# Sixteen partitions of one weight piece loaded from GpSimd's queue, dealt to chosen DMA engines

## The chip, the core and the metric

The kernel runs on one core of one Trainium2 chip. A core has five engines that run side by side, each with an instruction stream of its own: TensorE (PE in the profile; PEld is its loading of weights), VectorE (DVE), ScalarE (ACT), GpSimd (POOL) and SyncE (SP), which here does nothing but issue DMA transfers. The transfers themselves are carried out by 16 DMA engines, which all queues share. Engines wait for each other on semaphores. The metric is the time of one execution on the device, in microseconds (us); lower is better.

## The reference

One decoding step of a transformer block for two tokens (batch B = 2, one position each), everything in float32:

```
xn = layernorm(x)                                   # x: 2 x 512
q  = xn @ wq                                        # wq: 512 x 4096, 32 heads of 128
s[b,h,:] = q[b,h] . k_cache[b,h,:,:] / sqrt(128)    # 8192 cached positions per head
o[b,h]   = softmax(s[b,h,:]) @ v_cache[b,h,:,:]
s  = o @ wo                                         # wo: 4096 x 512
g  = silu( gelu(layernorm(xn) @ w1 + b1) @ w2 + b2 )   # 512 -> 1376 -> 512
out = x + s * g
```

The two caches are 268 MB each; with the weights, 559 MB are read once. wo, which this change is about, is 8 MB.

## The kernel before

**Tiling.** The 64 pairs of batch and head are taken two at a time, which gives N = 32 turns. The 128 partitions are two heads of 64 partitions each, with 128 cached positions per partition. A turn's K or V tile is then 128 partitions by 64 KB, 8 MB, and one transfer. K tiles go alternately to the buffers `kb0` and `kb1`, V tiles to the one buffer `vb`.

**A turn.** VectorE multiplies the K tile by the query (line 524) and sums over the head's 128 numbers (line 531), which gives the scores. The maximum is found over the partitions with the help of PE, ScalarE takes the exponentials into PZ (line 552), and PE multiplies PZ with the V tile, 64 matmul records a turn (line 575, tile `po`). ScalarE copies the product out (line 582). The maximum and the product of turn n are done while the scores of turn n + 1 are formed.

**The end.** The last turn's V tile does not go to `vb` but, in two halves, to `kb1`. When PE has done with `vb` for the last time, wo is loaded into it. wo lies as `wo_sb[partition, c, column]` with 32 rows c of 512 columns for each partition, cut by `WO_PIECES = (0, 16, 24, 29, 31, 32)` into pieces of 16, 8, 5 and 2 rows, and the last row in two parts of 384 and 128 columns. The pieces have semaphores of their own, so PE starts on each as it lands: the first 24 rows with 512 columns at once into `wide` (line 650, 48 records), the others into `acc` (line 659, 64 records). VectorE multiplies by the gate g and adds x (lines 667 and 668), SP stores the result (line 669) and waits until it has landed (line 125).

**What sets the order.** The program is a list of operations (`op`), each with the tiles that it reads and writes; `Plan` derives the waits from these and hands each engine its own operations in the order of the list. All transfers are issued by SP in that order (`load`, line 314), so that each waits until its buffer is free, and those behind it wait too. GpSimd sets four tiles at the start and does nothing after that. `busy` issues matmuls whose result nobody reads (line 562).

**What the change touches.** The loads of wo near the end of `decode_kernel`, the products into `wide`, three new tiles' declarations, and the final wait in `Plan.emit`.

Of the kernel before, what the change touches and what calls it, by code (L numbers as in the profile page):

```python
# [21 lines left out]
class Plan:  # L22
# [18 lines left out]
    def op(self, eng, fn, r=(), w=(), over=(), it=None, loop=False, dma=None):  # L41


        o = Op()
        o.eng, o.fn, o.it, o.loop, o.dma, o.tell = eng, fn, it, loop, dma, False
        need = {}

        def after(d, war):
            if d.dma is None and dma is None and d.eng == eng and (eng == "pe" or war):
                return  # L50
            if d.dma is None:
                if need.get(d.eng) is None or need[d.eng].idx < d.idx:
                    need[d.eng] = d
            else:
                k = ("dma", d.dma)
                if need.get(k) is None or need[k].idx < d.idx:
                    need[k] = d

        for k in r:
            if k in self.writer:  # L60
                after(self.writer[k], False)
        for k in list(w) + list(over):
            if k in self.writer:
                after(self.writer[k], False)
            for d in self.readers.get(k, ()):
                after(d, True)
        clock = self.clock[eng]
        need = {k: d for k, d in need.items() if clock.get(k, 0) < d.idx}
        o.deps = [(k, d) for k, d in need.items()
                  if not any(e is not d and e.done.get(k, 0) >= d.idx for e in need.values())]  # L70
        for _, d in o.deps:
            for k, v in d.done.items():
                clock[k] = max(clock.get(k, 0), v)
        own = eng if dma is None else ("dma", dma)
        self.count[own] = o.idx = self.count.get(own, 0) + 1
        o.done = dict(clock)
        o.done[own] = o.idx
        for k in w:
            self.writer[k] = o
            self.readers[k] = []  # L80
        for k in r:
            if k not in w:
                self.readers.setdefault(k, []).append(o)
        self.ops.append(o)

    def emit(self, heads):

        nc = self.nc
        for o in self.ops:
            for _, d in o.deps:  # L90
                d.tell = True
        sems, value, told = {}, {}, {}
        for o in self.ops:
            key = o.eng if o.dma is None else ("dma", o.dma)
            if key not in sems:
                sems[key] = nc.alloc_semaphore(o.eng if o.dma is None else f"dma_{o.dma}")

            step = 16 if o.dma is not None else int(o.tell or o.eng != "pe")
            told[key] = told.get(key, 0) + step
            value[id(o)] = told[key]  # L100
        for o in self.ops:
            o.waits = {k: value[id(d)] for k, d in o.deps}

        def put(o, waits, turn=None):
            e = self.eng[o.eng]
            for k, v in waits:
                e.wait_ge(sems[k], v)
            i = o.fn() if o.it is None else o.fn(o.it if turn is None else turn)
            if o.dma is not None:
                i.then_inc(sems[("dma", o.dma)], 16)  # L110
            elif o.tell or o.eng != "pe":
                i.then_inc(sems[o.eng], 1)

        def order(d):
            return sorted(d.items(), key=lambda kv: str(kv[0]))

        for e in self.eng:
            ops = [o for o in self.ops if o.eng == e]
            inside = [j for j, o in enumerate(ops) if o.loop]
            if not inside:  # L120
                for o in ops:
                    put(o, order(o.waits))
                if e == "sp":

                    nc.sync.wait_ge(sems[("dma", "out")], told[("dma", "out")])
                continue
            for o in ops[:inside[0]]:
                put(o, order(o.waits))
            turns = {}
            for j in inside:  # L130
                turns.setdefault(ops[j].it, []).append(ops[j])
            n, m = len(turns), len(turns[1])
            assert inside == list(range(inside[0], inside[-1] + 1)) and list(turns) == list(range(1, n + 1))
            assert all(len(t) == m for t in turns.values())


            body, ahead = [], {}
            for j in range(m):
                col = [turns[i][j] for i in range(1, n + 1)]
                assert len({o.tell for o in col[1:-1]}) == 1, j  # L140
                for o in col:
                    o.tell = col[1].tell
                ws = []
                for k in sorted(set().union(*(o.waits for o in col)), key=str):
                    if all(k not in o.waits for o in col[1:]):
                        ahead[k] = max(ahead.get(k, 0), col[0].waits[k])
                        continue
                    step = col[2].waits[k] - col[1].waits[k]
                    base = col[1].waits[k] - 2 * step
                    for o in col:  # L150
                        assert o.waits.get(k) == step * o.it + base or (o.it == 1 and k not in o.waits), \
                            (e, j, k, o.it, [x.waits.get(k) for x in col])
                    ws.append((k, step, base))
                body.append((col[1], ws))
            for k, v in order(ahead):
                self.eng[e].wait_ge(sems[k], v)
            et = self.eng[e].engine
            with nc.Fori(1, n + 1, 1, engines=bass.OrderedEngineSet([et]), head_slot={et: heads[e]}) as i:
                for o, ws in body:
                    put(o, [(k, i * step + base if base else i * step) for k, step, base in ws], i)  # L160
            for o in ops[inside[-1] + 1:]:
                put(o, order(o.waits))


def decode_kernel(nc, x, kc, vc, wq, wo, w1, b1, w2, b2, out):
    P = 128
# [10 lines left out]
    QT = 4  # L177
# [19 lines left out]
    op = plan.op  # L197
# [13 lines left out]
    def sbuf(name, shape):  # L211
        return nc.alloc_sbuf_tensor(name, shape, F32).ap()

    def psum(name, shape):
        return nc.alloc_psum_tensor(name, shape, F32).ap()
# [5 lines left out]
    vb = sbuf("vb", [P, KP * DH])  # L221
# [3 lines left out]
    wo_sb = vb.rearrange("p (c n) -> p c n", c=OC)  # L225
# [28 lines left out]
    q_nat = O4  # L254
    rl = sbuf("rl", [P, B])
    on = sbuf("on", [P, RM, OC])


    used = [0]
# [14 lines left out]
    at = used[0]  # L274
# [23 lines left out]
    wide = psum("wide", [P, D])  # L298
# [4 lines left out]
    def bank():  # L303
        i = turn[0] % 4
        turn[0] += 1
        return scratch[i], f"s{i}"
# [6 lines left out]
    def load(dst, src, sem, w, over=()):  # L313
        op("sp", lambda: nc.sync.dma_start(dst, src), (), w, over=over, dma=sem)  # L314
# [9 lines left out]

    WO_PIECES = (0, 16, 24, 29, 31, 32)
    WIDE = WO_PIECES[-4]
    CUT = D - P


# [51 lines left out]
    for j in range(QT):  # L381
        pe(lambda j=j: matmul(px[R * j:R * j + RM, :P], pick, x_sb[:, j * P:(j + 1) * P],
                              start=True, stop=True), ["pick", "x"], [kx])
# [92 lines left out]
    for i in range(NQ):  # L476
        for c in range(ND):
            wv = wq_sb[:, c, :].rearrange("p (h s d) -> p h s d", s=U, d=DH)
            a = (NQ - 1 - i) * B
            for j in range(QT):  # L480
# [4 lines left out]
                    start=(i + c == 0), stop=(i == NQ - 1 and c == ND - 1)),  # L485
                   ["xnT"] + [("kb", 0, s) for s in range(2)], ["po"])
    act(lambda: nc.scalar.copy(q_nat, PO), ["po"], ["o4"])
    for k in range(N // NB):

        b, e = divmod(k, HH // NB)  # L490
        i, g = divmod(e, GQ)
        p, kp = bank()
        for s in range(U):
            a = R * (U * g + s) + B * i + b
            pe(lambda p=p, s=s, a=a: matmul(p[HP * s:HP * (s + 1), :], ident[:, a:a + 1].to_broadcast([P, HP]), q_nat,
                                            start=True, stop=True), ["ident", "o4"], [kp])
# [121 lines left out]

    wo_r = wo.rearrange("(p c) n -> p c n", p=P)
    for i, (a, e) in enumerate(zip(WO_PIECES[:-1], WO_PIECES[1:-1])):  # L620
        load(wo_sb[:, a:e], wo_r[:, a:e], f"wo{i}", [("wo", i)], over=["vb"])
    for i, (a, e) in enumerate(((0, CUT), (CUT, D)), len(WO_PIECES) - 2):
        load(wo_sb[:, OC - 1, a:e], wo_r[:, OC - 1, a:e], f"wo{i}", [("wo", i)], over=["vb"])

    max_dve(N - 1)
    exps(N - 1)
# [17 lines left out]
    def piece(c, j=0):  # L644
        return ("wo", max(i for i, a in enumerate(WO_PIECES[:-1]) if a <= c) + int(c == OC - 1 and j * P >= CUT))


    for c in range(WIDE):
        j = c % QT
        pe(lambda c=c, j=j: matmul(wide[R * j:R * j + RM, :], on[:, :, c], wo_sb[:, c, :],  # L650
                                   start=(c < QT), stop=(c + QT >= WIDE)), ["on", piece(c)], ["wide"])
    w4 = O4
    act(lambda: nc.scalar.copy(w4, wide), ["wide"], ["o4"])

# [7 lines left out]
    for j in range(QT):  # L662
        pe(lambda j=j: matmul(acc[R * j:R * j + RM, :], mod[:, :RM], w4[:, j * P:(j + 1) * P], start=True, stop=False),
           ["mod", "o4"], ["acc"])
    rows(WIDE, OC)

# [32 lines left out]
```

## Time and profile before

| what | value |
|---|---|
| median of 3 runs | 1299.35 us (1299.26 to 1299.38) |
| profiled execution | 1299.24 us |
| span of its instructions | 1297.9 us |
| VectorE busy | 1134.3 us, 87% of the span |
| PE busy | 404.1 us, 31% |
| GpSimd busy | 1.4 us, 8 instructions |
| read from memory | 559.30 MB, 431 GB/s over the span |

The span runs from the first to the last instruction; the profiled execution's own time is 1.34 us longer. The profile gives for each stretch of time the engines' busy times, the mean busy share of the 16 DMA engines and the rate at which they moved bytes. A packet of the trace carries its size and time, but not the number of its DMA engine. Entries like `vb<-in_A_wo_dram` read as destination and source. "Us to landing" is the time from the issue of a transfer to its last byte, so it includes the time in the queue behind earlier transfers.

### The profile page before, as it was taken

What the parts mean: (1) busy time and instruction counts of PE and PEld (TensorE: products, weight loads), DVE (VectorE), ACT (ScalarE), POOL (GpSimd) and SP (SyncE); (2) the same over time, 40 slices, a digit from 0 to 9 for tenths busy, and PEclk for the clock granted to TensorE, in tenths of its full rate; (3) what the DMA queues carried; (4) which work ended last, traced back from release to release, by engine and by line L of the source; (5) the groups of instructions that cost most, each with busy time, mean ns of one, the idle gap of its engine ahead of it and who ended that gap; (6) DMA issues with size and microseconds to landing.
All of it is one profiled execution on the core that took longest, in us unless ns stands there. A gap on an engine that the chain in (4) does not pass through costs nothing.

```text
span 1297.9 us, 6789 instructions
## 1 busy us (share of the span) xinstructions
PE 404.1 (31%) x2728; PEld 122.4 (9%) x2728; DVE 1134.3 (87%) x276; ACT 77.7 (6%) x250; POOL 1.4 (0%) x8
## 2 busy tenths in 40 slices
PE   5603333312333311333321333321333321233337
PEld 1201110000101100101100101000001100001102
DVE  2499999988889988889988888988888988888991
ACT  1200000000000000000000000000000000000000
POOL 0000000000000000000000000000000000000000
PEclk9856666656666656666656666655666655666659
DMA  9999999999999999999999999999999999999998
GB/s 408 443 423 442 430 430 438 424 446 426 436 432 426 444 426 440 428 434 436 426 446 426 434 434 424 446 426 438 430 432 438 426 446 426 434 434 424 433 432 366
DMA packets 11087, 559.45 MB, mean 431 GB/s; under 512 B 1236, under 2 KB 1604, under 8 KB 1736
## 3 DMA queue, kind: packets, MB, share of 16 engines
q1 hardware_dynamic: 11080, 559.36, 99.7%
q8 instruction: 4, 0.07, 0.0%
q14 instruction: 3, 0.02, 0.0%
HBM read 559.30 MB, written 0.06 MB: 431 GB/s over the span
## 4 chain that ended last, share of the span: by engine, by line
DMA 68%; PE 24%; DVE 4%; issue 3%; ACT 0%; SPq 0%; DVEq 0%
DMA vb<-in_A_v_cache_dram 66%; PE po L575 21%; DMA vb<-in_A_wo_dram 2%; DVE sc L531 2%; DVE kb L524 1%; PE s L410 1%; DMA vb<-in_A_x_dram 1%; PE po L482 1%; PE s L452 0%; PE s L412 0%; PE acc L659 0%; DVE vb L418 0%; ACT L431 0%; PE s L459 0%; SPq L314 0%
## 5 line engine op out<-in xcount | busy, mean ns | idle before, releaser
L524 DVE TENSOR_TENSOR kb<-kb,Q 128x8192 f32<-128x8192 f32 x64 | 555.5, 8681 | 100.6 <-DMA kb<-in_A_k_cache_dram 91.4
L531 DVE TENSOR_REDUCE sc<-kb 128x64 f32<-128x8192 f32 x64 | 552.3, 8666 | 0.0
L575 PE MATMUL po<-vb,PZ 128*8 128x512 f32 x1984 | 280.7, 729 | 282.0 <-DMA vb<-in_A_v_cache_dram 279.4
L547 PE MATMUL s<-nm,srow 1*128 1x2 f32 x64 | 18.4, 355 | 359.5 <-DVE nm L541 359.5
L575 PEld LDWEIGHTS po<-vb,PZ 128*8 128x8 f32 x1984 | 56.3, 103 | 480.3 <-issue 477.5
L538 PE MATMUL s<-ident,mx 128*1 128x128 f32 x32 | 11.8, 369 | 203.6 <-DVE mx L535 203.6
L547 PEld LDWEIGHTS s<-nm,srow 1*128 1x128 f32 x64 | 15.7, 302 | 368.8 <-DVE nm L541 368.8
L582 ACT COPY o<-po 128x512 f32<-128x512 f32 x32 | 18.7, 585 | 521.6 <-PE po L575 521.6
L548 ACT COPY bias<-s 128x2 f32<-128x2 f32 x32 | 5.1, 160 | 628.2 <-PE s L547 628.2
L584 PE MATMUL s<-mod,o 128*128 128x2 f32 x256 | 33.6, 253 | 22.1 <-ACT o L582 22.1
L584 PEld LDWEIGHTS s<-mod,o 128*128 128x128 f32 x256 | 31.0, 191 | 51.4 <-ACT o L582 51.3
L552 ACT ACTIVATE PZ<-sc,bias 64x128 f32<-64x128 f32 x64 | 25.5, 399 | 1.8
L538 PEld LDWEIGHTS s<-ident,mx 128*1 128x1 f32 x32 | 2.5, 79 | 207.1 <-DVE mx L535 176.6
L590 DVE TENSOR_TENSOR Z<-blk,s 128x8 f32 (+1 forms) x32 | 5.2, 163 | 12.2 <-PE s L584 12.2
L418 DVE COPY vb<-vb 2x384 f32<-2x384 f32 x4 | 1.8, 501 | 15.9 <-ACT vb L414 15.9
L410 PE MATMUL s<-vb 128*2 128x512 f32 (+1 forms) x24 | 12.5, 675 | 0.3 <-ACT vb L375 0.3
L667 DVE TENSOR_TENSOR gate<-acc,gate 128x128 f32<-128x128 f32 x1 | 0.3, 291 | 13.3 <-PE acc L659 13.3
L552 ACT ACTIVATION_READ_ACCUMULATOR PZ<-sc,bias 64x1 f32 x64 | 11.8, 185 | 0.0
L535 DVE TENSOR_REDUCE mx<-sc 128x1 f32<-128x128 f32 x32 | 9.2, 286 | 1.1
L556 ACT ACTIVATE ZR<-half,rs 128x8 f32 (+1 forms) x32 | 9.6, 301 | 4.1
L541 DVE TENSOR_REDUCE nm<-s 1x2 f32<-1x128 f32 x32 | 8.7, 272 | 0.3 <-PE s L538 0.3
L575 PE MATMUL po<-kb,PZ 128*8 128x512 f32 x64 | 8.5, 686 | 1.4 <-ACT PZ L552 1.4
(88 smaller groups left out, 82.8 us busy)
## 6 DMA issues: line engine op xcount, KB each, us to landing
kb<-in_A_k_cache_dram SPq DMA_DIRECT2D x4, 4096.0 KB, 42.7
kb<-in_A_v_cache_dram SPq DMA_DIRECT2D x2, 4096.0 KB, 40.6
vb<-in_B_w_dram SPq DMA_DIRECT2D x2, 2752.0 KB, 12.2
vb<-in_A_wo_dram SPq DMA_DIRECT2D x1, 4096.0 KB, 20.2
vb<-in_A_wo_dram SPq DMA_DIRECT2D x1, 2048.0 KB, 24.7
vb<-in_A_wo_dram SPq DMA_DIRECT2D x1, 1280.0 KB, 27.3
vb<-in_A_wo_dram SPq DMA_DIRECT2D x1, 512.0 KB, 28.1
vb<-in_A_v_cache_dram SPq DMA_DIRECT2D x31, 29.5
```

The costliest lines, as they stand in the source:

```text
L410: pe(lambda f=f, w=w, ph=ph, c=c: matmul(ph[:B, :w], yT[:, c, :], w1_sb[:, c, f:f + w], start=(c == 0), stop=False), ["yT", "w1"], [k])
L482: pe(lambda i=i, c=c, wv=wv, a=a, j=j, hd=hd: matmul(PO[R * j:R * j + NQ * B, :].rearrange("m (h d) -> m h d", d=DH), xnT[:, c, a:a + NQ * ...
L524: vector(n, n, lambda n: nc.vector.tensor_tensor(out=k, in0=k, in1=cols(Q, n * DH, DH).unsqueeze(1).to_broadcast([P, M, DH]), op=ALU.mult) ...
L531: vector(n, n, lambda n: nc.vector.tensor_reduce(out=SC[:, s * M:(s + 1) * M], in_=k, axis=AX.X, op=ALU.add), [("kb", i, s)], [("sc", s)])
L535: vector(n, n, lambda n: nc.vector.tensor_reduce(out=MX, in_=SC, axis=AX.X, op=ALU.max), [("sc", 0), ("sc", 1)], ["mx"])
L538: pe(lambda i: transpose(PM[:1, :P], MX, ident), ["mx", "ident"], ["s1"], it=n, loop=n > 0)
L547: pe(lambda i: matmul(PN[:, :U], srow, NM, start=True, stop=True), ["srow", "nm"], ["s2"], **one)
L552: act(lambda i, r=r, s=s: nc.scalar.activation(PZ[r, :, s, :], sc[r], AF.Exp, bias=BIAS[r, s:s + 1], scale=SCALE, accum_out=RS[r]), ["bias ...
L556: act(lambda i: nc.scalar.activation(cols(ZR, i * UP - UP, UP), half, AF.Copy, scale=RS), ["half"] + [("rs", s) for s in range(U)], [("ZR" ...
L575: pe(lambda i, t=t, j=j, v=v: matmul(PO[R * j:R * j + U * JW, :], PZ[:, t].rearrange("p s j -> p (s j)"), v[:, t * JW:(t + 1) * JW, :].rea ...
L582: act(lambda i: nc.scalar.copy(O4, PO), ["po"], ["o4"], **one)
L584: pe(lambda i, k=k: matmul(PT[:, :U], O4[:, k * DH:(k + 1) * DH], mod[:, k:U * JW:JW], start=(k == 0), stop=(k == JW - 1)), ["o4", "mod"], ...
```

## The change

The first piece of wo (16 rows c of 512 columns, 32 KB a partition) is no longer one transfer over 128 partitions. SP loads partitions 0 to 111 of it. Partitions 112 to 127 are loaded by GpSimd in six transfers: seven partitions, six partitions, and the last three partitions in four quarters of 8 KB each. The list `DEAL` has a positive number for such a transfer and a negative one for a small load into a tile `unused`, whose data nobody reads. The numbers are chosen so that, if each transfer of n rows takes the next n of the 16 DMA engines in turn, the rows come out on particular engines; the sizes of the list add up to a multiple of 16. Counted that way from engine 0, the six skipped are 0 to 5, the seven rows go to 6 to 12, two are skipped (13, 14), the six rows go to 15 and 0 to 4, the quarters to 5 to 7, 8 to 10, 11 to 13 and 14, 15, 0, and 15 skipped lead back to 0.

Each of GpSimd's six transfers has a semaphore (`rest0` to `rest5`), and PE waits for all of them before it uses the first piece. Behind wo, SP issues 15 loads of 15 rows, 14 rows and so on down to one row of 128 bytes into a tile `marks`, which nobody reads either. At its end SP waits for these and for `unused` as well as for the stored result.

```diff
@@ Plan.emit @@
                 if e == "sp":
-                    nc.sync.wait_ge(sems[("dma", "out")], told[("dma", "out")])
+                    for k in ("mark", "unused", "out"):
+                        nc.sync.wait_ge(sems[("dma", k)], told[("dma", k)])
@@ decode_kernel @@
+    unused = sbuf("unused", [16, 8 * 8])
+    TAG = 32
+    marks = sbuf("marks", [P, 15 * TAG])
...
     WIDE = WO_PIECES[-4]
+    REST = 16
+    DEAL = (-6, 7, -2, 6, 3, 3, 3, 3, -15)
...
     for i, (a, e) in enumerate(zip(WO_PIECES[:-1], WO_PIECES[1:-1])):
-        load(wo_sb[:, a:e], wo_r[:, a:e], f"wo{i}", [("wo", i)], over=["vb"])
+        n = P if i else P - REST
+        load(wo_sb[:n, a:e], wo_r[:n, a:e], f"wo{i}", [("wo", i)], over=["vb"])
+    spare = [0]
+    def some(p, n, a, e, i):
+        op("pool", lambda: nc.gpsimd.dma_start(wo_sb[p:p + n, a:e], wo_r[p:p + n, a:e]), (), [("wo", "rest", i)],
+           over=["vb"], dma=f"rest{i}")
+    def skip(n):
+        i = spare[0]
+        spare[0] += 1
+        op("pool", lambda: nc.gpsimd.dma_start(unused[:n, i * 8:i * 8 + 8], wo_r[:n, 0, :8]), (), [("unused", i)],
+           over=["vb"], dma="unused")
+    cut, at, row = WO_PIECES[1], 0, P - REST
+    assert sum(abs(k) for k in DEAL) % 16 == 0
+    lo, step = 0, cut // 4
+    for k in DEAL:
+        if k < 0:
+            skip(-k)
+        elif k < P - row:
+            some(row, k, 0, cut, at)
+            row, at = row + k, at + 1
+        else:
+            some(row, k, lo, lo + step, at)
+            lo, at = lo + step, at + 1
+    assert lo == cut
+    RESTS = [("wo", "rest", i) for i in range(at)]
     for i, (a, e) in enumerate(((0, CUT), (CUT, D)), len(WO_PIECES) - 2):
         load(wo_sb[:, OC - 1, a:e], wo_r[:, OC - 1, a:e], f"wo{i}", [("wo", i)], over=["vb"])
+    for n in range(15, 0, -1):
+        load(marks[:n, (n - 1) * TAG:n * TAG], wq[:n, :TAG], "mark", [("mark", n)])
...
-                                   start=(c < QT), stop=(c + QT >= WIDE)), ["on", piece(c)], ["wide"])
+                                   start=(c < QT), stop=(c + QT >= WIDE)), ["on", piece(c)] + (RESTS if c < WO_PIECES[1] else []), ["wide"])
```

Lines move by the added ones: `load` goes from 314 to 318, the products into `wide` from 650 to 687, those into `acc` from 659 to 696, the store from 669 to 706.

GpSimd's stream, before, from its last instructions at the start of the program to its end (partitions x elements of a partition; 8192 elements are 32 KB):

```order
L343 MEMSET ident 128x128 [waits barrier_Pool_Activation_PE_DVE_SP_gather]
L344 ISA [waits pool]
L344 AFFINE_SELECT ident<-ident 128x128
L346 MEMSET vb 128x512
L347 MEMSET PZ 128x256
```

and with the change:

```order
L353 MEMSET vb 128x512
L354 MEMSET PZ 128x256
L639 DMA unused<-in_A_wo_dram 6x8 [waits pe]
L633 DMA vb<-in_A_wo_dram 7x8192
L639 DMA unused<-in_A_wo_dram 2x8
L633 DMA vb<-in_A_wo_dram 6x8192
L633 DMA vb<-in_A_wo_dram 3x2048 x4
L639 DMA unused<-in_A_wo_dram 15x8
```

Nine transfers now end the stream of GpSimd; the first waits for PE, as the first piece of wo does on SP.

SP's stream, before, from the last V tile's two halves to the end:

```order
L314 DMA kb<-in_A_v_cache_dram 128x8192 [waits dve] x2
L314 DMA vb<-in_A_wo_dram 128x8192 [waits pe]
L314 DMA vb<-in_A_wo_dram 128x4096
L314 DMA vb<-in_A_wo_dram 128x2560
L314 DMA vb<-in_A_wo_dram 128x1024
L314 DMA vb<-in_A_wo_dram 128x384
L314 DMA vb<-in_A_wo_dram 128x128
L669 DMA out_dram<-gate 112x128 [waits dve]
```

and with the change, up to the first of the 15 tiny loads:

```order
L318 DMA kb<-in_A_v_cache_dram 128x8192 [waits dve] x2
L318 DMA vb<-in_A_wo_dram 112x8192 [waits pe]
L318 DMA vb<-in_A_wo_dram 128x4096
L318 DMA vb<-in_A_wo_dram 128x2560
L318 DMA vb<-in_A_wo_dram 128x1024
L318 DMA vb<-in_A_wo_dram 128x384
L318 DMA vb<-in_A_wo_dram 128x128
L318 DMA marks<-in_A_wq_dram 15x32
```

The first piece has 112 rows in place of 128, and the 15 tiny loads stand between the last piece and the store.

PE's stream around its first products with wo, before:

```order
L636 MATMUL OA<-mod,Z 128x32 [waits dve]
L562 MATMUL s<-Q,ident 128x512 x3
L650 MATMUL wide<-vb,on 2x512 [waits dve,dma_wo0]
L650 MATMUL wide<-vb,on 2x512 x15
L650 MATMUL wide<-vb,on 2x512 [waits dma_wo1]
```

and with the change:

```order
L673 MATMUL OA<-mod,Z 128x32 [waits dve]
L569 MATMUL s<-Q,ident 128x512 x3
L687 MATMUL wide<-vb,on 2x512 [waits dma_rest4,dma_rest5,dma_rest3,dma_wo0,dma_rest2,dve,dma_rest1,dma_rest0]
L687 MATMUL wide<-vb,on 2x512 x15
L687 MATMUL wide<-vb,on 2x512 [waits dma_wo1]
```

The order of PE's work is the same; its first product with wo has six more waits.

## The prediction

> **What bounds the kernel now.** I read the page first, then the chain of waits from 1225 us on, then stretches of the last 40 us.
>
> The page of the kernel before, parts 2 and 4:
>
> ```profile
> DMA  9999999999999999999999999999999999999998
> GB/s 408 443 423 442 430 430 438 424 446 426 436 432 426 444 426 440 428 434 436 426 446 426 434 434 424 446 426 438 430 432 438 426 446 426 434 434 424 433 432 366
> ...
> DMA 68%; PE 24%; DVE 4%; issue 3%; ACT 0%; SPq 0%; DVEq 0%
> ```
>
> The 16 DMA engines are full in all 40 slices but the last. What the kernel loads cannot shrink by this change (the same 8 MB of wo are read), so the question is what the last slice does.
>
> Chain of waits, its end (start us, us, what):
>
> ```profile
> 1265.90 27.34 DMA vb<-in_A_wo_dram
> 1293.25 0.04 issue
> 1293.29 2.33 PE acc L659 x64
> 1295.62 0.02 issue
> 1295.64 0.30 DVE gate L667
> ```
>
> The end hangs on wo: its pieces are issued when the buffer vb comes free, the DMA queue needs until 1293.25 us for the first three, PE multiplies the rest as they land, and DVE and the store follow. The timeline of PE and SP there (start, duration, and in brackets the idle time before):
>
> ```profile
> 1265.06 2.96 SPq L314 DMA_DIRECT2D vb<-in_A_wo_dram  x6
> ...
> 1275.53 0.12 PEld L575 LDWEIGHTS po<-kb,PZ 128*8 128x8 f32 x8 [0.85 <-DMA kb<-in_A_v_cache_dram]
> ...
> 1285.31 3.62 PE L650 MATMUL wide<-vb,on 128*2 128x512 f32 x32 [0.74 <-DMA vb<-in_A_wo_dram]
> ...
> 1290.20 1.90 PE L650 MATMUL wide<-vb,on 128*2 128x512 f32 x16 [1.27 <-DMA vb<-in_A_wo_dram]
> ...
> 1295.02 0.29 PEld L659 LDWEIGHTS acc<-vb,on 128*2 128x2 f32 x8 [0.16 <-DMA vb<-in_A_wo_dram]
> ...
> 1296.29 0.35 SPq L669 DMA_DIRECT2D out_dram<-gate  x1
> ```
>
> So piece 0 lands at 1285.3, piece 1 at 1290.2, and the last waits for wo end near 1295.0. PE has only 0.74 and 1.27 us of idle time at the first two. Whatever delays the slowest DMA engine in the last pieces delays the end by as much.
>
> Stretches (us from the span's start, length, engines' busy times, then clock, DMA share, GB/s):
>
> ```profile
> 600.00:700.00 100.00, 30.56 (x219) 9.10 (x207) 89.04 (x19) 4.64 (x15) 0.00 (x0) 0.64 1.00 431
> 1264.10:1275.50 11.40, 7.45 (x55) 2.31 (x43) 4.39 (x4) 2.03 (x7) 0.00 (x0) 0.85 0.99 426
> 1275.50:1285.20 9.70, 9.07 (x60) 4.00 (x56) 0.56 (x3) 0.58 (x1) 0.00 (x0) 1.00 0.97 414
> 1293.20:1294.20 1.00, 0.91 (x37) 0.89 (x40) 0.00 (x0) 0.00 (x0) 0.00 (x0) 1.00 0.50 182
> 1294.20:1295.20 1.00, 1.00 (x38) 0.49 (x26) 0.00 (x0) 0.00 (x0) 0.00 (x0) 1.00 0.17 51
> ```
>
> In the steady part 431 GB/s over 16 engines is 26.9 GB/s each, with a share of 1.00: no engine loses anything to another. In the last 2 us the share falls to 0.50 and 0.17: some engines are done while a few still work. That is what dealing can win. The two shares are 0.67 us of work per engine; spread evenly it would end at 1293.9, some 1.3 us before 1295.2. **A gain is thus bounded by 1.3 us, 0.10%**, below the 0.2% (2.6 us of 1299.35) that a measurement of this kernel can tell from no change.
>
> **The change, part by part.**
>
> *Unit of price.* Piece 0 is 4096 KB in 128 rows, so a row is 32 KB, and at 26.9 GB/s one engine moves it in 1.22 us. Before, an engine has eight of them (9.7 us, the length of the stretch from 1275.50 to 1285.20).
>
> *Balance.* If the dealing works as written, every engine has seven rows from SP; counting the deal with its skipped engines, nine engines get 40 KB from GpSimd, four get 32 KB, and three get 8 KB. Three engines are thus lighter by 24 KB, 0.91 us, and nine heavier by 8 KB, 0.30 us. Whether the three are the late ones the trace does not show, since its packets carry no engine number. From -1.3 us (all of the loss above) to +0.3 us (the late ones among the nine); I take -0.3, since the heavier engines and the next latest take over soon.
>
> *The 112 rows.* Now an engine gets 7 rows and not 8, so the rows can no longer fall into the sixteen eights of every other load of vb and kb, and an engine can write next to partitions that another one is writing. The trace has one transfer over 112 rows, the final store:
>
> ```profile
> out_dram<-gate SPq DMA_DIRECT2D x1, 56.0 KB, 1.6
> ...
> q1 hardware_dynamic: 128, 0.06, 14.1%
> ```
>
> (the second row is that store's own stretch, 1296.3 to 1297.9: packets, MB, share of 16 engines). It is 512 bytes a row and goes the other way, so it says nothing on a collision of 32 KB rows. The bounds are therefore 0 (no row meets another; as in the 431 GB/s row) and all seven rows at half rate, 7 x 1.22 = 8.5 us. If a row meets one of another engine, the two share the way in and the later one is up to 1.22 us late. I take four meetings on the unluckiest engine, 4.9 us: a little over the middle, because an engine that is late goes on meeting the others' rows in the next pieces, and because only the worst of 16 engines counts.
>
> [...]
>
> *GpSimd's 16 rows.* The first real transfer sends seven neighbouring rows by seven engines at once, while SP's queue holds the last half of the V tile (which lands at 1275.5). [...] The lower bound is 0, since the bytes are only moved from one queue to another. [...]
>
> *Moved bytes.* GpSimd's rows overtake SP's backlog, 512 KB at 431 GB/s = 1.2 us. The V half of 1275.53 comes that much later, and PE's work behind it shifts by 1.2; 0.74 of it is eaten by the wait at 1285.31, the remaining 0.5 by the 1.27 at 1290.20. Without that cover it would be 1.2 us. Priced 0.
>
> *GpSimd's issuing.* Nine DMAs, waiting as SP does for PE to free vb. POOL issues none before; the nearest rows are SP's:
>
> ```profile
> L314 SPq DMA_DIRECT2D vb<-in_A_wo_dram x6: 328/428/435, 1265.1 to 1267.6; - x6
> ...
> SPq L669 <- DVE gate L668: 28.2, 1, 28.2
> ...
> L125 SPq EVENT_SEMAPHORE  x1: 17/17/17, 1297.9 to 1297.9; - x1
> ```
>
> (issue time in ns, min/median/max; SP's wait before the store; the wait that ends the program). At 0.43 us nine are 3.9 us, done by 1269. PE's first use is at 1285.31, so the eight up to the last row may take 20.2 / 8 = 2.5 us each before anything waits. Nothing is queued behind them on POOL. Priced 0, the slow case is a rival.
>
> *Six more waits* stand before PE's first product with wo; all PE work behind it waits for the latest of the seven pieces. Passed at once, each costs some 17 ns like the last row above, six 0.1 us; they stand in PE's idle 0.74 us. Priced 0.
>
> *Fifteen tiny loads.* 15 x 0.43 = 6.5 us of issuing on SP, from 1268.0 to 1274.5, inside its wait of 28.2 us for the store. They stand behind wo in the queue, at most 15 rows on one engine. By the store's row (14.1% of 16 engines over 1.6 us is 3.6 us for 128 packets, 28 ns each) 15 rows and 15 signals cost 0.85 us, after wo's last packet and before the store at 1296.29. Hidden; 0.85 us if the store had to queue behind them. The end's two added waits are for transfers that land before the store: 0.
>
> *Sum.* -0.3 + 4.9 + 2.4 = +7.0 us. The profiled execution took 1299.24 us (span 1297.9 and 1.34 around it), 0.11 under the median of 1299.35: **1306.3 us** against the median.
>
> **The rivals.**
>
> *Rows do not collide* (the other side: not slower). Place: piece 0, 1275.5 to 1285.2. Then only the balance term is left, 1299.35 - 0.3 = **1299.0**, between 1298.0 and 1299.7. It decides as soon as piece 0 lands by 1286.5 (1285.3 plus PE's 1.27 us) and the engines end no further apart than now. For it: every transfer in the trace moves at 26.9 GB/s per engine; against it: all of these but tiny ones have 128 rows, eight an engine.
>
> *GpSimd's rows come too late.* If each of the eight issues takes 3.5 us, not 0.43, the last is out at 1265.06 + 28 = 1293.1. PE's 48 products with wide (3.62 + 1.90 us) then end at 1298.6 in place of 1292.1, some 6.5 us later, which is nearly all seen at the end: **1305.8**. Below 2.5 us each it costs nothing. Nothing in the trace speaks for it but that POOL's price is unknown.
>
> *The dealing does not do what it says.* If each of GpSimd's transfers begins on the same first engine, the skipped loads move nothing, and three engines carry 32 + 32 + 4 x 8 = 96 KB where an even share is 32: 64 KB more, 2.4 us. On late engines that is +2.4, on the earliest (1.3 us ahead) +1.1: **1301.1** without collisions, within 0.2%. [...] No GpSimd transfer is in the trace to decide it.
>
> **How the numbers follow.** Collisions 0.55 (1306.3; its own range 1302 to 1314); no collisions 0.30; GpSimd late 0.06; wrong dealing 0.07; an unforeseen gain 0.02. Slower by over 0.2%: collisions nearly whole (0.54), late GpSimd, and a tail of the dealing: 0.61. Within 0.2%: 0.37. Faster: 0.02, since the balance cannot give 2.6 us. The top of collisions is all bounds together, 8.5 + 4.9 + 0.3 = 13.7 us, 1313.0. To hold 8 in 10 the range reaches over the case without collisions: 1298.6 to 1313.
>
> **What would show it.** For the 112 rows: piece 0 (then 3584 KB) lands well after 1285.3, the DMA share between 1275 and 1290 falls below 0.9, and the stretch in which it fades at the end grows from 2 us to 5 or more. For GpSimd's rows: the V half of 1275.53 comes over 1.2 us later. For the issuing: POOL's nine DMAs spread over more than 20 us, and PE's wait before wide names one of them. For the dealing: how far the tiny loads, of 15 engines down to one, land apart. I am wrong if piece 0 lands at 1285 to 1286 and the end is where it was, or if the loss stands with PE waiting for GpSimd while SP's pieces are in time.

## The result, and the profile after

The changed kernel takes **1318.9 us** (median of four runs, 1317.64 to 1319.58); the kernel before, on the same chip, 1299.37 (1299.26 to 1299.41). The ratio is 1.0149, 95% interval 1.0132 to 1.0167: 19.5 us slower. The profiled execution took 1318.48 us with a span of 1317.2. The direction was forecast, and so was the kind of loss, rows that get in each other's way; the sum itself, +7.0, is little over a third of what came, and the time lies outside the range.

The page of the kernel after, parts 2, 3 and 4:

```profile
DMA  9999999999999999999999999999999999999997
GB/s 422 419 441 422 440 442 422 442 432 430 442 420 442 436 428 440 420 442 442 422 442 428 434 442 420 442 432 432 440 420 442 438 426 440 426 436 430 434 337 208
...
q0 software_dynamic: 288, 0.53, 0.3%
...
DMA 70%; PE 25%; DVE 3%; issue 1%; ACT 0%; POOL 0%; SPq 0%; DVEq 0%
```

The busy share reads as before: nines, and one digit lower at the end. What fell is the rate beside it: the last two slices (33 us each) move 337 and 208 GB/s, where the kernel before had 432 and 366. The engines are as occupied as before and move less. GpSimd's queue, which was not there before, moved 0.53 MB.

Stretches of the kernel after, cut where the last V half, piece 0 from SyncE, and the last piece land (start and end, length, busy us of PE, PEld, DVE, ACT, POOL, then clock, DMA share, GB/s):

```profile
1264.40:1282.80 18.40, 8.15 (x55) 2.44 (x47) 4.34 (x4) 2.03 (x7) 4.73 (x9) 0.86 1.04 284
1282.80:1301.80 19.00, 11.54 (x56) 4.23 (x56) 0.56 (x3) 0.58 (x1) 0.00 (x0) 0.77 0.95 218
1301.80:1307.60 5.80, 2.71 (x16) 0.59 (x20) 0.00 (x0) 0.00 (x0) 0.00 (x0) 0.50 0.97 391
1307.60:1312.70 5.10, 4.39 (x44) 0.77 (x36) 0.00 (x0) 0.58 (x1) 0.00 (x0) 0.92 0.34 124
```

In the first two, 37 us long together, the share is 1.04 and 0.95 and the rate 284 and 218 GB/s. (The share adds up the packets' own times; where it passes 1, packets of one engine must have overlapped.) From 1301.8 on the rate is 391 again: the loss belongs to the V half and piece 0, while GpSimd's rows and the 112 rows are under way, and hardly to what follows.

The timeline of PE and SP in the kernel after:

```profile
1265.62 2.97 SPq L318 DMA_DIRECT2D vb<-in_A_wo_dram  x6
1268.64 33.66 SPq L318 DMA_DIRECT2D marks<-in_A_wq_dram  x15
...
1282.87 6.12 PE L582 MATMUL po<-kb,PZ 128*8 128x512 f32 x32 [6.69 <-DMA kb<-in_A_v_cache_dram]
...
1304.88 7.07 PE L687 MATMUL wide<-vb,on 128*2 128x512 f32 x48 [10.47 <-DMA vb<-in_A_wo_dram]
...
1315.53 0.34 SPq L706 DMA_DIRECT2D out_dram<-gate  x1
```

and the DMA issues of its last part (issuer, KB each, median us from issue to landing):

```profile
vb<-in_A_wo_dram SPq DMA_DIRECT2D x1, 3584.0 KB, 36.2
...
vb<-in_A_wo_dram POOLq DMA_DIRECT2D x1, 224.0 KB, 16.0
vb<-in_A_wo_dram POOLq DMA_DIRECT2D x1, 192.0 KB, 25.3
...
vb<-in_A_wo_dram POOLq DMA_DIRECT2D x4, 24.0 KB, 33.3
...
vb<-in_A_wo_dram SPq DMA_DIRECT2D x1, 64.0 KB, 44.6
...
unused<-in_A_wo_dram POOLq DMA_DIRECT2D x1, 0.2 KB, 6.8
```

So the delay builds up as follows. The V half lands at 1282.87 in place of 1275.53, **7.3 us late**. Piece 0 is issued at 1265.62 and lands 36.2 us later, at 1301.8 in place of 1285.3: 16.5 late, **9.2 more**. The last piece, the sixth of SyncE's issues, starts at 1268.2 and lands 44.6 us later, by 1312.8 in place of 1295.2: some 17.5 late, **1.0 more**. The store is issued at 1315.53 in place of 1296.29, 19.24 late, which is all of the difference between the two profiled executions (1318.48 less 1299.24): **1.7 more**, and for these the chain of waits shows the way:

```profile
1267.57 2.03 POOL vb L633 x4
1269.60 34.94 DMA vb<-in_A_wo_dram
1304.54 0.35 issue
1304.88 7.12 PE wide L687 x48
...
1312.67 0.40 PE acc L700 x8
1313.07 1.79 PE acc L696 x64
```

PE waits with its first product until 1304.54, when GpSimd's last quarter of three rows lands, 2.7 us after SyncE's piece 0. It then runs the 48 products in one go, 7.07 us where the two groups of before took 3.62 + 1.90, since the granted clock was 0.50 up to 1307.6 (third stretch). The end no longer waits for wo's last piece but for PE, which comes out of its first group of products too late to keep up.

### The profile page after: what moved, and what is told of

It is laid out like the page before. It is cut to its first block, busy times and chain, and to the rows that moved or that the text cites. A ratio compares the mean times of both kernels' runs of the same rounds, so it can differ in the third digit from the quotient of the medians.

```text
span 1317.2 us, 6817 instructions
## 1 busy us (share of the span) xinstructions
PE 414.4 (31%) x2728; PEld 124.0 (9%) x2728; DVE 1134.3 (86%) x276; ACT 77.7 (6%) x250; POOL 6.1 (0%) x17
## 4 chain that ended last, share of the span: by engine, by line
DMA 70%; PE 25%; DVE 3%; issue 1%; ACT 0%; POOL 0%; SPq 0%; DVEq 0%
DMA vb<-in_A_v_cache_dram 66%; PE po L582 22%; DMA vb<-in_A_wo_dram 3%; DVE kb L531 1%; DVE sc L538 1%; PE s L417 1%; DMA vb<-in_A_x_dram 1%; PE wide L687 1%; PE po L489 1%; PE s L459 0%; PE s L419 0%; POOL vb L633 0%; PE acc L696 0%; DVE vb L425 0%; ACT L438 0%
## 5 line engine op out<-in xcount | busy, mean ns | idle before, releaser
L582 PE MATMUL po<-vb,PZ 128*8 128x512 f32 x1984 | 288.9, 748 | 287.5 <-DMA vb<-in_A_v_cache_dram 286.2
L545 PE MATMUL s<-ident,mx 128*1 128x128 f32 x32 | 11.8, 369 | 189.8 <-DVE mx L542 189.8
L554 PEld LDWEIGHTS s<-nm,srow 1*128 1x128 f32 x64 | 15.7, 302 | 370.9 <-DVE nm L548 370.9
L597 DVE TENSOR_TENSOR Z<-blk,s 128x8 f32 (+1 forms) x32 | 5.2, 163 | 21.8 <-PE s L591 21.8
L425 DVE COPY vb<-vb 2x384 f32<-2x384 f32 x4 | 1.8, 500 | 14.7 <-ACT vb L421 14.7
L582 PE MATMUL po<-kb,PZ 128*8 128x512 f32 x64 | 11.4, 879 | 8.1 <-DMA kb<-in_A_v_cache_dram 6.7
L559 ACT ACTIVATION_READ_ACCUMULATOR PZ<-sc,bias 64x1 f32 x64 | 11.8, 185 | 0.0
L687 PE MATMUL wide<-vb,on 128*2 128x512 f32 x48 | 7.1, 751 | 10.5 <-DMA vb<-in_A_wo_dram 10.5
## 6 DMA issues: line engine op xcount, KB each, us to landing
vb<-in_A_wo_dram SPq DMA_DIRECT2D x1, 3584.0 KB, 36.2
```

What stands on the lines that cost most here:

```text
L545: pe(lambda i: transpose(PM[:1, :P], MX, ident), ["mx", "ident"], ["s1"], it=n, loop=n > 0)
L554: pe(lambda i: matmul(PN[:, :U], srow, NM, start=True, stop=True), ["srow", "nm"], ["s2"], **one)
L559: act(lambda i, r=r, s=s: nc.scalar.activation(PZ[r, :, s, :], sc[r], AF.Exp, bias=BIAS[r, s:s + 1], scale=SCALE, accum_out=RS[r]), ["bias ...
L582: pe(lambda i, t=t, j=j, v=v: matmul(PO[R * j:R * j + U * JW, :], PZ[:, t].rearrange("p s j -> p (s j)"), v[:, t * JW:(t + 1) * JW, :].rea ...
```

## The experiments

The kernel before stood between 1299.40 and 1299.47 us beside all of these; differences are against the run on the same chip. Each variant was run once, marks_only ten times; 13 runs of the kernel before on one chip lie between 1299.33 and 1299.67, so 0.1 us is no difference here; the changed kernel's four runs lie 1.9 apart.

**Lone transfers.** The kernel before, with loads behind its store, each issued when the one before has landed:

```diff
+    def one(eng, k, lo, hi, step=1, c=16):
+        e = nc.sync if eng == "sp" else nc.gpsimd
+        op(eng, lambda: e.dma_start(quiet[lo:hi:step, :c], wo_r[lo:hi:step, :c]), last[0], [("q", k)], over=free, dma=f"q{k}")
+        last[0] = [("q", k)]
+    one("sp", 0, 0, 128, 1)
+    one("sp", 1, 0, 112, 1)
+    one("sp", 2, 0, 64, 1)
...
+    for k in range(8):
+        lo = (0, 4, 8, 12, 64, 68, 72, 76)[k]
...
```

(the loop at its end has GpSimd load rows lo and lo + 1, without a wait between the eight)

> The kernel before, and behind its stored result twelve transfers of 32 KB rows of wo into the buffer kb0, each waiting for the one ahead, so that each runs alone; then eight transfers of two rows issued by GpSimd without a wait between them. Nothing of the result changes; the total time is not compared. [...] For the dealing: eight transfers of two rows take some 7 us if each goes on to the next engines, some 19 us if all of them begin on the same engine.

Stretches of this kernel: 128 rows, 112 rows, 64 rows from SyncE, and the eight pairs from GpSimd; then GpSimd's timeline for the pairs:

```profile
1298.50:1310.40 11.90, 0.00 (x0) 0.00 (x0) 0.00 (x0) 0.00 (x0) 0.00 (x0) 0.60 0.86 352
1310.60:1326.90 16.30, 0.00 (x0) 0.00 (x0) 0.00 (x0) 0.00 (x0) 0.00 (x0) 0.50 0.86 225
1327.00:1339.70 12.70, 0.00 (x0) 0.00 (x0) 0.00 (x0) 0.00 (x0) 0.00 (x0) 0.50 0.78 165
...
1387.30:1402.20 14.90, 0.00 (x0) 0.00 (x0) 0.00 (x0) 0.00 (x0) 4.09 (x8) 0.50 0.11 35
```

```profile
1387.39 4.09 POOL L694 DMA_DIRECT2D kb<-in_A_wo_dram  x8 [6.76 <-DMA kb<-in_A_wo_dram]
```

With nothing beside them, 112 rows take 4.4 us longer than 128, though seven rows an engine for eight would by themselves be 1.2 us shorter (an estimate, at 1.22 us a row): same share of 0.86, 225 in place of 352 GB/s. 64 neighbours take longer than 128 rows. The 112 rows therefore need no late engine and no other queue to be slow: the loss is inside the one transfer. The eight pairs are issued in 4.09 us, but the last lands 14.7 us after the first issue, at a share of 0.11, which is under two of 16 engines (0.11 x 16 = 1.8). The pairs do not run side by side, as they would on sixteen different engines. Either all eight begin on the same engines, and the count that the dealing relies on does not move on, or the queue takes them one after another; this run alone does not tell which. GpSimd's lone pairs took 3.7 us for rows 0 and 64, 4.5 for 0 and 1, and 4.9 for 0 and 32.

**One part alone.** Three kernels, each with one piece of the change in the kernel before:

```diff
-        load(wo_sb[:, a:e], wo_r[:, a:e], f"wo{i}", [("wo", i)], over=["vb"])
+        n = P if i else P - 16
+        load(wo_sb[:n, a:e], wo_r[:n, a:e], f"wo{i}", [("wo", i)], over=["vb"])
```

(the first piece with 112 rows, the 16 left out)

> The kernel before with wo's first piece loaded over 112 partitions by SP; the other 16 partitions are not loaded at all (512 KB fewer; the products with them use what the last V tile left there), no GpSimd transfers, no tiny loads. Theory (112 rows collide): 2 to 8 us over the kernel before. Rival (only the sixteen rows of GpSimd disturb): 1.2 us under it, as 512 KB fewer are moved.

```diff
+        if i == 0:
+            load(wo_sb[:64, a:e], wo_r[:64, a:e], "wo0", [("wo", 0)], over=["vb"])
+            load(wo_sb[64:, a:e], wo_r[64:, a:e], "wo0b", [("wo", "b")], over=["vb"])
+            continue
```

(the first piece in two halves of 64 neighbours)

> The kernel before with wo's first piece loaded in two transfers, partitions 0 to 63 and 64 to 127, both by SP; the same bytes, 32 KB rows, four rows per engine in each. [...] Rival (engines do not disturb each other): no change, 1299.4.

```diff
+        e -= 0 if i else 2
...
+    other = kb[0].rearrange("p (c n) -> p c n", c=OC)
+    free = [("kb", 0, h) for h in range(2)]
...
+        op("pool", lambda: nc.gpsimd.dma_start(other[p:p + n, a:e], wo_r[p:p + n, a:e]), (), [("wo", "rest", i)],
+           over=free, dma=f"rest{i}")
```

(the first piece with 128 rows of 28 KB, the last 4 KB of each left out, and the nine transfers of GpSimd beside it into another buffer, onto the same partitions; PE does not wait for these)

> SP loads 14 of the first piece's 16 rows c over all 128 partitions (the last two are left out, and the products with them use what the last V tile left there), and GpSimd carries out its nine transfers as in the changed kernel, but into partitions 112 to 127 of the buffer kb0, which PE does not wait for; so the bytes are those of the changed kernel and only GpSimd's rows leave the usual split. No tiny loads. Theory (both parts collide): 3 to 10 us over the kernel before. Rival A (only the 112 rows cost): within 1 us of it. Rival B (GpSimd's transfers alone are the loss): 15 to 20 us.

They took 1306.61 (+7.2), 1312.19 (+12.8) and 1312.49 (+13.1). The stretch behind the V half in each, in this order:

```profile
1277.50:1292.80 15.30, 9.04 (x56) 4.00 (x56) 0.56 (x3) 0.59 (x1) 0.00 (x0) 0.88 0.94 263
```

```profile
1278.00:1298.20 20.20, 9.04 (x56) 4.00 (x56) 0.56 (x3) 0.59 (x1) 0.00 (x0) 0.85 0.96 212
```

```profile
1279.70:1296.80 17.10, 10.73 (x56) 4.26 (x56) 0.56 (x3) 0.59 (x1) 0.00 (x0) 0.81 0.96 272
```

All three show a share of 0.94 to 0.96 at 212 to 272 GB/s, as the changed kernel does. The 112 rows cost 7.2 us although 512 KB, an estimated 1.2 us, are not read: 8.4 in all. GpSimd's rows beside an undivided piece 0 cost 13.1 us, and together with 8.4 that is 21.5. In the changed kernel the last piece lands 17.5 us late (PE adds the last 1.7 behind it): the two parts overlap by some 4 us and otherwise add up. deal_aside came out dearer than the 3 to 10 of its theory. two_halves lies 3.1 over the 9.7 us that it would cost if each half took as long as the whole piece did before; there the V half already lands 2.5 us late, at 1278.0 in place of 1275.5. (PE runs its 48 products in one go in 7.37 us where before they took 5.52, but that hardly shows at the end: the last piece of wo itself lands 12.7 us late.)

**Which rows, or how many?** Lone loads again, of eleven shapes:

> The kernel before with eleven lone loads from SyncE behind the store, each issued when the one before has landed, 32 KB a row: rows 0-127, 0-119, 0-111, 0-95, 0-63, every second row, 0-31, every fourth row, 0-15, every eighth row, and rows 0, 7, ... 105. A lone 128 rows took 12.0 us, eight rows of 1.22 us one after another and 2.2 us of fixed time; 64 neighbours took 12.8, 16 neighbours 6.6. [...] Rival: only the number of rows matters, whatever lies between them: every second row takes the 12.8 of 64 neighbours, every eighth the 6.6 of 16.

The DMA issues of this kernel, one window for each transfer. In order: rows 0-127, 0-119, 0-111, 0-95, 0-63, every second row, 0-31, every fourth, 0-15, every eighth, every seventh (KB, us from issue to landing):

```profile
kb<-in_A_wo_dram SPq DMA_DIRECT2D x1, 4096.0 KB, 12.1
kb<-in_A_wo_dram SPq DMA_DIRECT2D x1, 3840.0 KB, 21.8
kb<-in_A_wo_dram SPq DMA_DIRECT2D x1, 3584.0 KB, 17.2
kb<-in_A_wo_dram SPq DMA_DIRECT2D x1, 3072.0 KB, 16.4
kb<-in_A_wo_dram SPq DMA_DIRECT2D x1, 2048.0 KB, 12.7
kb<-in_A_wo_dram SPq DMA_DIRECT2D x1, 2048.0 KB, 7.7
kb<-in_A_wo_dram SPq DMA_DIRECT2D x1, 1024.0 KB, 7.1
kb<-in_A_wo_dram SPq DMA_DIRECT2D x1, 1024.0 KB, 5.1
kb<-in_A_wo_dram SPq DMA_DIRECT2D x1, 512.0 KB, 6.6
kb<-in_A_wo_dram SPq DMA_DIRECT2D x1, 512.0 KB, 4.9
kb<-in_A_wo_dram SPq DMA_DIRECT2D x1, 512.0 KB, 4.8
```

64 rows take 12.7 us as neighbours and 7.7 as every second row; 32 rows take 7.1 or 5.1, 16 rows 6.6 or 4.8. What matters is which rows they are. 96, 112 and 120 neighbours need 16.4, 17.2 and 21.8 us, more than the 12.1 of all 128; no run shows why. GpSimd's lone pairs, measured once each, differ too: rows 0 and 64 were the quickest (3.7 us), rows 0 and 1 (4.5) and 0 and 32 (4.9) slower. One rival is left: in every load here the rows read from memory change along with the partitions written, and no run moves only one of the two. That the rows of wo lie badly in memory is thus not excluded, but the pairs speak against mere distance in memory, as rows 32 apart come out worse than neighbours and rows 64 apart better.

In place, the pair to two_halves, the first piece split by even and odd rows:

```diff
+            load(wo_sb[0::2, a:e], wo_r[0::2, a:e], "wo0", [("wo", 0)], over=["vb"])
+            load(wo_sb[1::2, a:e], wo_r[1::2, a:e], "wo0b", [("wo", "b")], over=["vb"])
```

> [...] Theory: within 1 us of the kernel before (1299 to 1301). Rival, that any piece other than one of 128 rows makes engines late: 1308 to 1313, as two_halves (1312.2).

It took 1299.56 us (+0.1), where the halves of neighbours cost 12.8. Its stretches to the landing of the V half and of piece 0:

```profile
1264.20:1275.50 11.30, 7.04 (x43) 2.31 (x39) 4.58 (x4) 2.03 (x7) 0.00 (x0) 0.74 1.00 430
1275.50:1285.50 10.00, 10.00 (x67) 4.21 (x60) 0.56 (x3) 0.58 (x1) 0.00 (x0) 0.95 0.97 416
```

Two pieces for one and an added wait are thus free, and two pieces of 64 rows, the even and the odd, are together as fast as one of 128 (416 GB/s against 414). And a first piece with eight rows fewer:

```diff
+        n = P if i else P - 8
+        load(wo_sb[:n, a:e], wo_r[:n, a:e], f"wo{i}", [("wo", i)], over=["vb"])
```

> The kernel before with wo's first piece loaded over 120 partitions by SP (8 partitions are not loaded, 256 KB fewer, and the products with them use what the last V tile left there); no GpSimd transfers, no tiny loads. [...] Rival (the odd number of seven rows is what costs in the 112-row piece): within 2 us of the kernel before, as the engines in use have eight rows each.

1311.16 us (+11.8), more than the 7.2 of 112 rows, though only 256 KB are left unread here and 512 there; the lone 21.8 and 17.2 us stand in the same order. The lone 120 rows came in 135 packets, 15 of them under 512 bytes, and the lone 112 in 128, 16 of them under 512. If there is one such packet for each engine in use, an estimate from these counts, 120 rows are eight on each of 15 engines.

**GpSimd's part.** First the same amount (512 KB) by GpSimd in one load over all 128 rows; SyncE's first piece is that much smaller, and PE waits for both:

```diff
+    op("pool", lambda: nc.gpsimd.dma_start(wo_sb[:, 14:16], wo_r[:, 14:16]), (), [("wo", "rest", 0)],
+       over=["vb"], dma="rest0")
```

> SP loads 14 of the first piece's 16 rows c over all 128 partitions and GpSimd the other two (512 KB, 4 KB a partition) over all 128 partitions in one transfer; PE waits for both before its first product with wo, no tiny loads. The same bytes come from GpSimd's queue as in the changed kernel, but every engine has eight partitions again, as in the other loads. Theory (only a split other than the usual one costs): within 1 us of the kernel before. Rival (GpSimd's queue beside SP's is what slows the engines): 10 us or more over it.

1299.47 us, as before. Its stretches:

```profile
1264.20:1276.50 12.30, 9.18 (x63) 2.86 (x55) 4.56 (x4) 2.03 (x7) 0.66 (x1) 0.72 0.97 417
1276.50:1285.50 9.00, 9.00 (x60) 4.05 (x56) 0.56 (x3) 0.58 (x1) 0.00 (x0) 1.00 1.00 424
```

Half a megabyte from a second queue at the same time costs nothing here. Then deal_aside again, with the rows of each transfer four apart, taken from partitions 0 to 24 in place of 112 to 127:

```diff
-        op("pool", lambda: nc.gpsimd.dma_start(other[p:p + n, a:e], wo_r[p:p + n, a:e]), (), [("wo", "rest", i)],
+        op("pool", lambda: nc.gpsimd.dma_start(other[p:p + 4 * n:4, a:e], wo_r[p:p + 4 * n:4, a:e]), (), [("wo", "rest", i)],
```

> [...] Theory (meeting rows are the loss): only the unequal load is left, 64 KB too much on three engines, 2.4 us: 1301 to 1302. Rival (many transfers from GpSimd beside SP's queue are the loss): 1312 as before.

1301.0 us (+1.5) where the neighbours cost 13.1, at full rate:

```profile
1264.20:1275.70 11.50, 8.46 (x55) 2.84 (x51) 4.51 (x4) 2.03 (x7) 4.73 (x9) 0.70 1.00 429
1275.70:1286.50 10.80, 9.99 (x68) 4.18 (x60) 0.56 (x3) 0.58 (x1) 0.00 (x0) 1.00 0.99 418
```

Both kernels have the same nine transfers from the same queue at the same time with the same bytes; 11.6 of the 13.1 us hang on which rows they are. Which engine carries which row no trace shows. That the loss goes down to 1.5 us, inside the 1.1 to 2.4 that the prediction gives for unequal shares, fits the case that every transfer of GpSimd begins on the same first engine. Then the changed kernel with its 16 rows in one transfer, and with the dealing but no skipping loads:

```diff
-    for k in DEAL:
...
+    some(P - REST, REST, 0, WO_PIECES[1], 0)
```

> The changed kernel with GpSimd's sixteen partitions in one transfer of 16 rows of 32 KB, one row an engine, in place of nine transfers; the tiny loads stay. Theory (rows that meet): the 112 rows alone cost 7.2 us with 512 KB fewer, so some 8 with them, and the sixteen rows, which took 7.0 us on their own in place of some 3.5, 3 to 4 more: 1310 to 1313. Rival (the dealing that always begins on the same engines is most of the loss): 1307 to 1308. Rival (the number of transfers does not matter): 1318 as in the changed kernel.

```diff
-    DEAL = (-6, 7, -2, 6, 3, 3, 3, 3, -15)
+    DEAL = (7, 6, 3, 3, 3, 3)
```

> The changed kernel without the three small loads of GpSimd that are to move the dealing on (6, 2 and 15 rows of 32 bytes); its six real transfers follow each other. Theory (each of GpSimd's transfers begins on the same first engine whatever went ahead): the rows go to the same engines as in the changed kernel, 1317 to 1319. Rival (the dealing goes on from where the last transfer ended): then the six transfers' 25 shares go round all engines, no engine gets more than 40 KB, and the time is near that of the single transfer of sixteen rows, 1312.

They took 1312.28 (+12.8) and 1318.67 (+19.3, inside the changed kernel's own 1317.64 to 1319.58). So nine transfers cost 6.6 us more than one, though the V half lands as late with one (1282.8). Without the three loads that are there to move the deal along, the time stays. The way to it does not quite, as a PE row and an issue row of no_skips show:

```profile
1287.92 5.26 PE L582 MATMUL po<-kb,PZ 128*8 128x512 f32 x32 [11.94 <-DMA kb<-in_A_v_cache_dram]
...
vb<-in_A_wo_dram SPq DMA_DIRECT2D x1, 64.0 KB, 46.6
```

The V half is 12.4 us late, not 7.3, and the last piece, issued at 1268.0, some 19.4, not 17.5; in exchange PE adds nothing behind it. The equal time is therefore a weaker sign than it looks. It fits the theory that the three move nothing along (the rival gave 1312), but they do shift what lands when.

**The tiny loads.** The 15 of them alone, in the kernel before:

```diff
+    for n in range(15, 0, -1):
+        load(marks[:n, (n - 1) * TAG:n * TAG], wq[:n, :TAG], "mark", [("mark", n)])
```

> The kernel before with the fifteen tiny loads behind wo and the wait for them at the end, nothing else. Theory of the prediction (hidden under SP's wait): 1299.4, within 0.2 us. Rival (each tiny load takes some 0.2 us on its engine, as the spacing of the landings in the changed kernel suggests, 3 us on the engine that has all fifteen, and the store queues behind): 1300 to 1302.

1299.5 us against 1299.47, ratio 1.0001 (0.9991 to 1.001). SP in this kernel:

```profile
1268.91 15.70 SPq L317 DMA_DIRECT2D marks<-in_A_wq_dram  x15
...
1296.46 0.34 SPq L675 DMA_DIRECT2D out_dram<-gate  x1
```

Their issuing takes 15.7 us, over the 6.5 worked out, but ends 11.9 us before the store. Why it takes longer no run shows; a full queue is a guess.

## Why the prediction was right and wrong

- **What bounds the kernel** was right: the end hangs on the last pieces of wo, and the loss came through them, with the share near 1 and the rate down.
- **The 112 rows**, priced at +4.9 of 0 to 8.5: right in kind, too small. The place measured 7.2 with an estimated 1.2 us of reading left out, 8.4, hardly below the upper bound. "Four meetings on the unluckiest engine" took a collision for an accident of timing; lone 112 rows at 225 GB/s show that it comes with such a transfer. That two rows that meet share a way in was the author's assumption; no trace shows where rows meet. The rival that rows do not collide, given 0.30, falls with sp112_alone.
- **GpSimd's 16 rows**, +2.4 in the sum and 4.9 among its bounds: this is the step that failed. No run shows either figure; deal_aside measured 13.1 for these rows alone. The estimate looked at the first real transfer, of seven rows, and left out that the writers also hold up the V half's rows (4.2 us late in deal_aside, 7.3 in the changed kernel), and that six more rows and three in quarters follow. Nor does this loss fall together with that of the 112 rows by much: some 4 of the 13.1 us do, and the other 9 are still nearly twice the 4.9. Even all the bounds together, +13.7, stay below the 19.5. (The range of collisions is given once as up to 1314, while these bounds give 1313.0; neither reaches 1318.9.)
- **Balance**, -0.3: a gain never appeared. The even shares most likely did not come about (next point), and no run here has them, so whether the 1.3 us at the end can be won stays open.
- **The dealing does not do what it says**, a rival given 0.07: the eight pairs (14.7 us at a share of 0.11), deal_own_ways (+1.5) and the time of no_skips (1318.67) fit it, though no trace numbers the engines, so it is not shown. Nor does any run show that a transfer takes the next engines in turn, on which the list DEAL counts. Its price was right (1.1 to 2.4 worked out, 1.5 in deal_own_ways), but it stood as an alternative to collisions, and the runs fit both at once.
- **Moved bytes**, 0: the 1.2 us of GpSimd's overtaking are hidden, as pool128 shows, where the same 512 KB overtake and the time stays.
- **Issuing**, 0: nine DMAs took 4.73 us on POOL, 0.53 each against the 0.43 taken. But the rival "GpSimd late" looked only at the issue. Issued by 1270.6, the quarters landed 33.3 us later, and PE's first product waited 2.7 us for the last of them. By the landings above this makes up to 1.7 of the 19.5 us; no run took it away alone.
- **Six more waits**, 0: even_odd and pool128 add one wait each, at +0.1 and 0; six were not tried alone. **Tiny loads**, 0: right.

What stays open is why the lone transfers of 96, 112 and 120 rows are slower than that of all 128, and why 120 is the worst; the trace does not number the engines. Open too, as said above, is whether it is the partitions written or the rows read that matter.

## What to carry to other kernels

Where DMA is the bound, look at GB/s beside the busy share: a share of 0.95 at 218 GB/s, as here, where it was 0.97 at 414 before, means that the engines are held up while they move data. Cut a full-width load along the free axis (pool128, no loss) or by every second row, rather than into blocks of neighbouring partitions (0.1 against 12.8 us here for the same amount in two halves). And when several terms of lateness hit a queue that is already full, do not let one stand for the other: of 8.4 and 13.1 only some 4 us fell together here.

## What the runs showed that was not expected

- A lone load of 120 neighbouring rows takes 21.8 us, 1.8 times the 12.1 of all 128.
- Beside SyncE's full queue GpSimd's transfers are slow however small: 192 bytes took 6.8 us, seven rows 16.0 and the quarters of 24 KB, behind them in the queue, 33.3, where seven lone rows took 6.4. The full queue is only part of it: in deal_own_ways, at full rate, the three took 6.7, 8.3 and 16.3 us.
- SyncE's issuing of 15 tiny loads is not fixed: 15.7 us in marks_only, 33.66 in the changed kernel, where six issues of wo took 2.97.
